# Another written-out order for a gated linear attention with a maxout layer

## The chip, the core and the metric

The kernel runs on one core of a Trainium2 chip. A core has TensorE (PE, the matmuls), VectorE (DVE), ScalarE (ACT) and GpSimd (POOL), each with an instruction stream of its own that runs in its own order; the streams wait for each other by semaphores. All DMAs of this kernel are issued by SyncE (SP), also in one order. The time is that of the device for one execution, in microseconds (us). The kernel before takes 144.04 us (median of three runs, 143.94 to 144.6).

## The reference

There are four batches of 768 tokens and eight heads of 48 channels. For each head a state of 48 x 48 is decayed by alpha, takes in the product of k and v, and is read by q. Then a layer takes the largest of three products of the 384 channels and multiplies it with a last weight:

```
for t in range(S):
    state = alpha[:, :, t, :, None] * state + einsum('bhd,bhe->bhde', k[:, :, t], v[:, :, t])
    y[:, :, t] = einsum('bhd,bhde->bhe', q[:, :, t], state)
x = y, heads side by side                    # 3072 x 384
h = maximum(maximum(x @ w1, x @ w2), x @ w3) # 3072 x 768
out = h @ w_out                              # 3072 x 384
```

## The kernel before

The tokens are worked through in 12 steps of 256 tokens (two units of 128); a step takes 256 tokens of one batch, and steps s and s+4 are neighbours in the same batch. Within a unit the recurrence is done in chunks by matmuls: the products of decayed q and k give a matrix of scores that is masked and multiplied with v, and the state that came into the unit adds its share. Two tokens at a time are folded into a pair, so the decay is summed over pairs. The maxout is done as x @ w1 + max(0, x @ (w2 - w1), x @ (w3 - w1)): the weights are subtracted once, w1 @ w_out is multiplied once, and TensorE adds x @ (w1 @ w_out) to the product of the maxima with w_out.

Nothing schedules the work at run time. A string, `ORDER`, lists about 760 pieces, and `emit` (line 538) issues each piece's instructions to their engines in that order. So the string sets, for each engine, the order of its own stream, the engine that does a movable piece, and the PSUM banks. A piece is written

```
k0v@3      piece k, index 0, on VectorE, of step 3   (v VectorE, p GpSimd, a ScalarE)
G2@4#7     piece G, index 2, of step 4, into PSUM bank 7
H5@0#3     five warming matmuls on a tile of zeros, into bank 3
```

The pieces, by the engine that they can go to, with the line of the instruction:

- SyncE: l loads alpha, q, k or v of a step in the index's order alpha 0, k 1, q 2, v 3 (line 102, 384 KB each, four buffers each); K loads a weight column group (118, 121); J loads the constants (130); D transposes q and k by a DMA (290, steps 5 to 11); W stores (500).
- ScalarE alone: N and r the logarithm of alpha and the inverse (209, 214, 216), e, f and g the decays from the sums (240, 250), I the row mask.
- TensorE: c sums the decays (231, 234), T transposes q and k (283, steps 0 to 4), A the scores (304), Y the outputs of a step (330), S the update of the state (388), B and P work on the weights (429, 440), G the gate products (452, six matmuls each), O the output products (486), H warming matmuls (505).
- VectorE alone: a the masks (319; 315 for step 0), the second maximum h1, h3, h5 (461), most state additions s (400).
- VectorE or GpSimd: m alpha products of a pair (205), u and w the near factors of k and q (219, 222), k and q the scaling by the decays (260), z the decay of the state (404), d the weight differences (418), M the gates between units (377).
- Any that can: x copies a step's outputs (162 or 164), v copies values by unit, y spreads the state, t copies what T made, b, n, C, p copy weights; h0, h2, h4 the first maximum (463 or 465), o scales an output (168 or 170), V scales v (168).

The weights are loaded into buffers of later steps: K0 to K7 lie in the third and fourth buffers of alpha, q, k and v, so that l0@2 can't be issued until K0 has been read. The waits between pieces follow from the tiles that they share. A piece that comes earlier in the string than another on the same engine runs earlier there; the string says nothing of the order between engines.

Of the kernel before, what the change touches and what calls it, by code (L numbers as in the profile page):

```python
# [23 lines left out]
def kernel(  # L24
# [513 lines left out]
    def emit(order):  # L538
# [21 lines left out]
        T1@2#5 t1v@2 K10@0 l1@4 h0a@1 b2a@0 G1@1#6 h1v@1 K11@0 K9@0 G3@1#1 l0@3 V0a@2 r0a@4 v1a@2 A1@2#3,7 a2v@2  # L560
        A0@2#0,2 a0v@2 a3v@2 S0@2#5,4 s0a@2 a1v@2 B2@0#6 n2v@0 G4@1#3 G4@0#0 G5@1#7 l0@5 z0p@2 l2@4 h3v@1 v0a@2
        Y0@2#5 x0v@2 Y2@2#2 y0a@2 Y3@2 x1a@2 M1p@0 u0p@4 k0v@4 G5@0#6 h4a@0 h5v@0 G5@2#1 l1@3 C2a@0 C0v@0 l2@3
        G4@2#5 l3@3 r1a@4 C1a@0 h4v@2 z1p@0 y1a@0 G0@2#2 m0v@3 s1v@2 h4a@1 G2@2#0 h2v@2 h5v@1 h5v@2 h0a@2 P0@0#6
        P1@0#5 N0a@3 r0a@3 p1a@0 w0v@4 q0v@4 c0@3#4 P2@0#3 e0a@3 m0p@5 G1@2#0 M0p@4 N0a@5 c0@5#7 f0a@3 r0a@5
        r1a@3 p0a@0 u0v@3 k0p@3 p2a@0 G3@2#1 h3v@2 f0a@5 T0@4#2 t0v@4 g0a@5 e0a@5 g0a@3 l3@4 T1@4#5 t1v@4 O0@0#6
        l0@7 l0@6 A1@4#3,1 h1v@2 V0a@3 a2v@4 M0p@5 w0p@3 q0v@3 A0@4#2,7 o0a@0 l1@5 S0@3#4,5 s0a@3 M1p@1 M0v@3
        z0p@3 l1@6 l2@5 O1@0#0 a1v@4 r1a@5 V0a@4 a3v@4 s1v@3 T0@3#3 t0v@3 o1a@0 T1@3#6 t1a@3 z1p@1 O0@1#4 m0p@7
        a0v@4 o0v@1 l0@8 y0a@3 N0a@7 A1@3#7,1 A0@3#5,3 l3@5 v0a@3 S0@4#0,6 W0@0 s0v@4 a1v@3 a0v@3 a2v@3 v0p@4
        m0p@6 N0a@6 O0@2#2 v1a@3 y1a@1 w0v@5 o0a@2 z0p@4 u0p@5 s1v@4 c0@7#4 v1p@4 c0@6#0 O1@1#3 r0a@7 o1a@1
        g0a@7 l0@9 g0a@6 Y3@3#5 a3v@3 Y2@3 Y0@3#7 r0a@8 x0a@3 Y0@4#2 Y2@4#6 l1@7 y0p@4 Y1@4 Y3@4 x1v@4 x0v@4  # L570
        O1@2#3 o1v@2 m0v@8 k0v@5 f0a@6 W1@0 l2@6 G0@4#1 h0v@4 e0a@6 x1a@3 M0p@6 G4@3#7 h4v@3 G2@3#6 G1@3#2
        G3@3#3 h2v@3 h3v@3 G4@4#1 l3@7 W0@2 q0p@5 D0@5 V0a@5 f0a@7 M1p@2 v1a@5 r1a@8 r0a@6 u0p@6 N0a@8 m0p@9
        r1a@6 c0@8#0 G0@3#5 e0a@8 h0a@3 r1a@7 h1v@3 G5@3#7 h5v@3 w0p@6 k0p@6 q0v@6 l3@6 D1@5 G5@4#6 G3@4#3 N0a@9
        V0a@7 h4a@4 h5v@4 e0a@7 c0@9#5 f0a@9 e0a@9 M1p@3 g0a@8 u0p@7 G2@4#2 h2a@4 f0a@8 g0a@9 M0p@8 G1@4#7 h1v@4
        O0@3#1 z1v@2 y1a@2 h3v@4 S0@5#6,4 s0v@5 k0p@7 r0a@9 A0@5#2,0 a1v@5 D1@6 W0@1 D0@6 z0v@5 A1@5#5,7 a2v@5
        a3v@5 o0a@3 V0a@6 l2@7 W0@3 O1@3#3 a0v@5 o1v@3 O1@4#6 y0a@5 o1a@4 r1a@9 v0p@7 v0p@5 Y0@5#0 Y1@5 v0v@6
        s1v@5 x0v@5 Y2@5#5 Y3@5 x1a@5 l0@10 S0@7#7,1 M1p@4 M0p@7 z1p@3 s0v@7 z0p@7 W1@1 l3@8 A1@6#2,3 a2v@6
        a3v@6 A0@6#6,4 a1v@6 S0@6#0,5 s0v@6 G2@5#7 G3@5#2 h2a@5 h3v@5 a0v@6 y0a@7 w0p@7 M1p@5 q0p@7 l1@8 D0@7
        D1@7 l2@8 G4@5#3 h4a@5 G1@5#4 G0@5#0 h0v@5 m0p@10 N0a@10 y1p@3 M0p@9 G5@5#7 O0@4#2 o0a@4 z1p@4 z0p@6
        y0a@6 c0@10#6 e0a@10 f0a@10 h1v@5 h5v@5 O1@5#3 O0@5#0 v1v@7 v1v@6 Y2@6#2 l0@11 s1v@6 u0v@8 k0v@8 g0a@10  # L580
        M1v@6 M0v@10 V0a@8 o1a@5 v0v@8 Y3@6 x1v@6 Y1@6#4 Y0@6 l2@9 r0a@10 S0@8#7 A0@7#5,6 s1v@7 a1v@7 s0v@8
        A1@7#3,2 a3v@7 a0v@7 a2v@7 x0a@6 G2@6#1 h2a@6 G3@6#6 h3v@6 G5@6#7 W1@3 G0@6#2 h0v@6 w0p@8 y1a@4 m0p@11
        z0p@8 N0a@11 W0@4 Y3@7#5 Y2@7 x1v@7 l1@9 W1@2 l3@9 Y0@7#3 Y1@7 x0a@7 c0@11#4 e0a@11 q0p@8 D0@8 D1@8
# [12 lines left out]
        h4a@11 h4a@10 G5@10#1 G2@11#5 h5v@10 o1a@8 W1@8 G3@11#0 h2v@11 h3v@11 W0@8 G0@11#2 h0v@11 G1@11#3 h1v@11
        G5@11#4 O1@10#7 O2@11#1 o1a@10 W1@10 h5v@11 O0@10#6 o0a@10 O3@11 o0v@11 O4@11#5,0 W0@10 W0@11 O5@11
        o1a@11 W1@11 O6@11 o2v@11 W2@11
    """

    blank = hTs[NH - 1].rearrange("p j m -> p (j m)")[:, :512]
# [34 lines left out]
```

## Time and profile before

| | us |
|---|---|
| median of the runs | 144.04 |
| the profiled execution | 143.54 |
| its span, first to last instruction | 141.8 |
| TensorE busy | 132.4 |
| VectorE busy | 113.7 |
| ScalarE busy | 95.5 |
| GpSimd busy | 73.8 |

The span is 1.7 us shorter than the profiled execution's time, since the launch and the end of the program lie outside it. Busy times of different engines lie beside each other. A view by time gives a start, a duration, the engine, the line, the operation and its tiles, and in brackets how long the engine had been idle before and what released it. TensorE's clock is granted by a throttle, and the profile gives it as a share of full speed.

### The profile page before, as it was taken

Reading aid. Unit: us, or ns where it says so; the run is one execution under the profiler, and the core shown is the slowest. Engines: PE = TensorE matmul, PEld = TensorE weight load, DVE = VectorE, ACT = ScalarE, POOL = GpSimd, SP = SyncE. Lnnn points to the kernel's source line nnn. Section 1 sums busy time; section 2 is a strip of 40 time slices with the busy share of each in tenths; the row PEclk is TensorE's granted clock in tenths of the full one; section 3 lists DMA queues with packets and bytes.
Section 4 is the critical chain, followed back from the end, with each engine's and each line's share of the span. In section 5 each row is a group of like instructions: output and inputs, shape, how many; then the busy total and the mean of one; then the engine's idle time right before and its main releaser. Section 6 shows DMA issues by size and latency. Waiting matters only on the chain.

```text
span 141.8 us, 5323 instructions
## 1 busy us (share of the span) xinstructions
PE 132.4 (93%) x2236; PEld 96.6 (68%) x2236; DVE 113.7 (80%) x215; ACT 95.5 (67%) x202; POOL 73.8 (52%) x107
## 2 busy tenths in 40 slices
PE   6988887999999999979999999899999999999990
PEld 2434556798868675768758858687678865788770
DVE  5466979989997999498999899977789879866711
ACT  3496798999899989996975486497375541344111
POOL 8217078257335399759495935888629643200000
PEclk9999996899999999999999999999999999999999
DMA  4999999999999998969999999998997955620214
GB/s 107 312 344 325 306 332 269 277 333 361 263 271 249 282 310 253 322 201 109 219 204 274 254 190 332 320 143 182 202 260 199 196 112 161 244 97 16 96 72 150
DMA packets 73031, 32.42 MB, mean 229 GB/s; under 512 B 65456, under 2 KB 73008, under 8 KB 73008
## 3 DMA queue, kind: packets, MB, share of 16 engines
q1 hardware_dynamic: 73008, 32.09, 86.4%
q8 instruction: 17, 0.28, 0.8%
q14 instruction: 6, 0.05, 0.1%
HBM read 23.69 MB, written 4.72 MB: 200 GB/s over the span
## 4 chain that ended last, share of the span: by engine, by line
PE 75%; SPq 8%; DVE 7%; DMA 4%; ACT 2%; issue 2%; DVEq 0%
PE bank L452 32%; PE bank L486 23%; PE bank L330 8%; SPq L102 5%; DMA rv<-in_v_dram 4%; PE bank L304 4%; PE bank L388 2%; SPq L118 2%; PE bank L440 2%; PE bank L283 2%; DVE lat L319 1%; DVE hT L461 1%; ACT qkT L162 1%; DVE qk L260 1%; PE bank L231 1%
## 5 line engine op out<-in xcount | busy, mean ns | idle before, releaser
L452 PE MATMUL bank<-xT,wdif 128*128 128x256 f16 x432 | 50.8, 275 | 0.8 <-DVE h L463 0.8
L452 PEld LDWEIGHTS <-wdif 128*128 128x128 f16 x432 | 41.4, 98 | 6.8 <-issue 1.1
L319 DVE TENSOR_TENSOR lat<-bank,cb 128x512 f16<-128x512 f32 x44 | 28.0, 681 | 1.3 <-PE bank L304 1.2
L461 DVE TENSOR_TENSOR hT<-bank,h 128x512 f16<-128x512 f32 x36 | 23.9, 685 | 6.2 <-PE bank L452 3.2
L486 PE MATMUL bank<-wo,hT 128*128 128x384 f16 (+1 forms) x150 | 27.5, 320 | 0.0
L486 PEld LDWEIGHTS <-hT 128*128 128x128 f16 x150 | 14.5, 98 | 8.9
L168 ACT ACTIVATE ob<-bank,ca 128x384 f32<-128x384 f32 (+1 forms) x18 | 10.3, 570 | 14.2 <-PE bank L486 12.9
L465 ACT ACTIVATE h<-bank 128x512 f16<-128x512 f32 x21 | 12.2, 599 | 8.1 <-PE bank L452 7.8
L486 PE MATMUL bank<-w1o,xT 128*128 128x384 f16 (+1 forms) x75 | 15.9, 321 | 0.0
L260 POOL TENSOR_TENSOR qk<-rk,ic 128x768 f16<-128x768 f32 x6 | 11.5, 1920 | 4.7 <-DVE rk L219 3.3
L505 PE MATMUL bank<-hT 128*128 128x512 f16 x42 | 12.7, 440 | 1.4 <-DVE hT L603 1.2
L168 ACT ACTIVATE vt<-rv,ca 128x768 f16<-128x768 f32 x12 | 11.3, 945 | 3.2 <-DMA rv<-in_v_dram 3.2
L162 ACT CAST xT<-bank 128x384 f16<-128x384 f32 x16 | 7.5, 480 | 7.1 <-PE bank L330 7.1
L222 POOL TENSOR_TENSOR rq<-rq,ic 128x384 f32<-128x384 f32 x8 | 8.0, 999 | 7.4 <-DMA rq<-in_q_dram 4.3
L463 DVE TENSOR_SCALAR h<-bank 128x512 f16<-128x512 f32 x15 | 9.9, 680 | 1.2 <-PE bank L452 1.2
L164 POOL COPY vu<-vt 64x384 f16<-64x384 f16 x14 | 7.3, 520 | 5.2 <-ACT vt L168 4.7
L205 POOL TENSOR_TENSOR ra<-ra 128x384 f32<-128x384 f32 x7 | 7.5, 1075 | 3.3 <-DMA ra<-in_alpha_dram 3.2
L162 ACT CAST st<-kept 64x192 f16<-64x192 f32 x26 | 9.0, 347 | 0.3
L260 POOL TENSOR_TENSOR qk<-rq,ac 128x768 f16<-128x768 f32 x5 | 9.1, 1814 | 0.1
L330 PE MATMUL bank<-lat,vu 128*32 128x128 f16 x352 | 8.3, 224 | 0.8 <-issue 0.7
L486 PEld LDWEIGHTS <-xT 128*128 128x128 f16 x75 | 6.5, 98 | 3.1
L505 PEld LDWEIGHTS <-hT 128*128 128x128 f16 x42 | 4.2, 110 | 6.4 <-issue 3.2
(80 smaller groups left out, 219.2 us busy)
## 6 DMA issues: line engine op xcount, KB each, us to landing
ra<-in_alpha_dram SPq DMA_DIRECT2D x12, 384.0 KB, 5.3
rk<-in_k_dram SPq DMA_DIRECT2D x12, 384.0 KB, 5.3
rq<-in_q_dram SPq DMA_DIRECT2D x12, 384.0 KB, 5.3
rv<-in_v_dram SPq DMA_DIRECT2D x12, 384.0 KB, 5.7
out_dram<-ob SPq DMA_DIRECT2D x23, 192.0 KB, 3.2
wst<-in_moe_w_out_dram SPq DMA_DIRECT2D x3, 384.0 KB, 7.2
ra<-in_moe_w_dram SPq DMA_DIRECT2D x2, 384.0 KB, 5.9
rk<-in_moe_w_dram SPq DMA_DIRECT2D x2, 384.0 KB, 5.5
```

The costliest lines, as they stand in the source:

```text
L162: nc.scalar.copy(out=dst, in_=src)
L168: nc.scalar.mul(dst, src, col)
L222: engines[eng].tensor_mul(raw("q", s, 0), raw("q", s, 0), decays["k"][s % 3][:, 0])
L260: engines[eng].tensor_mul(dst, src, by)
L319: nc.vector.tensor_mul(lats[s % 2][u][:, i], bank(("aps", s, u, i), [HP, P]), pmask.unsqueeze(1).broadcast_to([P, HP, P]))
L330: nc.tensor.matmul(y[x][C * m:C * (m + 1), f, :], lhs, rhs, start=(s, x, m) not in begun, stop=(seen[x] or U * (s // B) + x == 0) and n == ...
L452: nc.tensor.matmul(gps[:, j, :], wdif[:, f, g, jj * P:(jj + 1) * P], xT[:, f].rearrange("p u t -> p (u t)"), start=(f == 0), stop=(f == NF ...
L461: nc.vector.tensor_max(hTs[s % NH][:, 2 * jg:2 * jg + 2, :], gps, h)
L463: nc.vector.tensor_scalar_max(h, gps, 0.0)
L465: nc.scalar.activation(out=h, in_=gps, func=AFT.Relu)
L486: nc.tensor.matmul(ops, lhs, (w1o if what == "x" else wo16)[:, j, cols], start=((what, j) == every[0]), stop=((what, j) == every[-1]))
L505: nc.tensor.matmul(wps, blank[:, :P], blank, start=True, stop=True)
```

## The change

The string is replaced as a whole; the program around it is the same. The same pieces of work are in it (45 warming matmuls in place of 42). What differs is the place of each piece in its engine's stream, the banks, and the engine of some sixty movable pieces. The new string comes from a further search, which works each candidate through in the order of time and lets VectorE and GpSimd exclude each other, the one that is there first going ahead.

The engine's share of the movable pieces changes as follows (pieces before and after):

```
            VectorE    GpSimd    ScalarE
k            6 -> 9     6 -> 3
q            7 -> 8     5 -> 4
d            2 -> 4     4 -> 2
u            7 -> 5     5 -> 7
w            4 -> 5     8 -> 7
v            7 -> 4     7 -> 9     8 -> 9
z            4 -> 6    16 -> 14
M            3 -> 7    17 -> 13
y                       5 -> 7    13 -> 11
x            8 -> 5               16 -> 19
h           51 -> 50              21 -> 22
o            7 -> 5               18 -> 20
s           17 -> 16               3 -> 4
b            0 -> 2                3 -> 1
n            2 -> 1                1 -> 2
```

The first part of the string, the parts around the later steps that are named below, and the end, before (-) and after (+):

```diff
     ORDER = """
-        l0@0 m0v@0 r0a@0 N0a@0 r1a@0 J1@0 l1@0 u0v@0 H15@0#0 c0@0#0 e0a@0 k0v@0 K0@0 b0a@0 f0a@0 J0@0 I0a@0
-        H5@0#1 B0@0#1 l2@0 w0v@0 g0a@0 q0v@0 H6@0#2 T0@0#2 M0p@0 l0@1 m0p@1 r0a@1 N0a@1 K2@0 d1v@0 H3@0#3 c0@1#3
-        e0a@1 g0a@1 K1@0 d0p@0 r1a@1 T1@0#4 t1v@0 t0a@0 H3@0#5 H2^t1@0#5 A1@0#5,6 l1@1 u0v@1 k0v@1 l2@1 w0v@1
-        f0a@1 q0v@1 A0@0#7,0 a0v@0 a2v@0 a1v@0 l3@0 a3v@0 n0a@0 V0a@0 l3@1 V0a@1 v1p@1 v0p@1 K3@0 H5@0#4
-        S0@0#4,2 T0@1#3 t0a@1 T1@1#7 t1a@1 H2@0#5 S0@1#5,0 b1a@0 s0v@1 s0a@0 l0@2 m0v@2 N0a@2 K4@0 H1@0#6
-        A0@1#6,1 a0v@1 a1v@1 A1@1#3,7 a3v@1 M0p@1 z0p@1 y0a@1 a2v@1 z0p@0 d2p@0 y0a@0 B1@0#5 n1v@0 K5@0 d3v@0
-        s1v@0 l0@4 m0v@4 l2@2 c0@2#4 l1@2 g0a@2 M0p@2 Y0@0#6,1 x0a@0 Y3@0 x1a@0 K7@0 K6@0 r0a@2 r1a@2 w0p@2
-        Y2@1#7 Y3@1 x1a@1 s1v@1 f0a@2 d4p@0 G1@0#3 N0a@4 l3@2 K8@0 d5p@0 Y0@1#5 u0v@2 e0a@2 q0v@2 G0@0#2 h0a@0
...
-        z0p@8 N0a@11 W0@4 Y3@7#5 Y2@7 x1v@7 l1@9 W1@2 l3@9 Y0@7#3 Y1@7 x0a@7 c0@11#4 e0a@11 q0p@8 D0@8 D1@8
...
-        G3@7#6 G4@7#4 h4v@7 l3@10 h2v@7 h5v@7 h3v@7 O0@6#7 o0a@6 O1@6#0 D1@9 A0@8#2,3 a0v@8 A1@8#4,1 a2v@8 o1v@6
...
-        o1a@7 W1@7 G3@10#3 x1a@11 G0@10#5 G2@10#2 o0v@8 G1@10#0 h0v@10 G4@10#7 h1v@10 h2a@10 h3v@10 G4@11#4
-        h4a@11 h4a@10 G5@10#1 G2@11#5 h5v@10 o1a@8 W1@8 G3@11#0 h2v@11 h3v@11 W0@8 G0@11#2 h0v@11 G1@11#3 h1v@11
-        G5@11#4 O1@10#7 O2@11#1 o1a@10 W1@10 h5v@11 O0@10#6 o0a@10 O3@11 o0v@11 O4@11#5,0 W0@10 W0@11 O5@11
-        o1a@11 W1@11 O6@11 o2v@11 W2@11
+        K0@0 b0v@0 J0@0 H13@0#0 B0@0#0 l0@0 l0@1 J1@0 m0p@0 m0v@1 l1@0 l2@0 I0a@0 K1@0 N0a@0 H6@0#1 c0@0#1 r0a@0
+        l1@1 n0v@0 K2@0 f0a@0 e0a@0 r0a@1 l2@1 u0v@0 k0v@0 l3@1 N0a@1 r1a@0 w0v@0 H6@0#2 c0@1#2 e0a@1 q0v@0
+        H5@0#3 T1@0#3 l3@0 d0v@0 g0a@1 T0@0#4 u0v@1 t1a@0 t0a@0 d1v@0 l0@2 k0v@1 g0a@0 l0@4 f0a@1 H2@0#5
+        H2^t1@0#5 A0@0#5,6 r1a@1 K3@0 V0a@1 w0v@1 q0v@1 A1@0#7,0 a2v@0 H5@0#3 S0@1#3,4 T1@1#1 K4@0 v0p@1 K5@0
+        V0a@0 m0p@2 l2@2 a1v@0 a3v@0 l1@2 t1a@1 s0a@1 T0@1#2 t0v@1 S0@0#7,6 s0a@0 M0v@1 H2@0#0 A1@1#0,1 z0p@1
+        N0a@2 M0v@0 z0v@0 A0@1#3,2 y0a@0 K6@0 a0v@0 s1v@0 v1p@1 y0a@1 a0v@1 H2@0#7 Y3@0#7 Y0@0#5 a3v@1 r0a@2
+        r1a@2 K7@0 c0@2#6 s1v@1 b1v@0 H2@0#3 B1@0#3 x0a@0 m0p@4 N0a@4 d2v@0 x1a@0 c0@4#1 g0a@4 g0a@2 M1p@0 d3v@0
+        l3@2 a1v@1 e0a@2 G2@0#4 G0@0#5 f0a@2 n1a@0 M0p@2 M0p@4 K8@0 a2v@1 G1@0#7 e0a@4 l2@4 h0a@0 u0v@2 k0v@2
+        Y0@1#2 x0a@1 Y2@1#6 Y3@1 x1a@1 G3@0#3 l0@3 G0@1#0 r0a@4 r1a@4 h0a@1 w0p@2 q0v@2 G2@1#5 b2a@0 h1v@0
+        T1@2#2 h2v@1 h2a@0 f0a@4 d4p@0 t1v@2 T0@2#6 B2@0#0 G1@1#7 h3v@0 V0a@2 t0v@2 n2a@0 K10@0 l1@4 G3@1#5
...
+        c0@11#2 G3@6#6 a3v@7 o1a@5 a2v@7 Y3@7#0 w0v@8 Y2@7 o0a@5 Y0@7#7 Y1@7 x1a@7 q0v@8 D0@8 G5@6#1 x0a@7
+        G0@7#5 G3@7#3 g0a@11 e0a@11 y1a@4 D1@8 G1@7#0 w0p@9 q0p@9 v0p@8 k0v@9 h4a@6 V0a@9 h3v@6 z0v@8 G4@7#7
+        r1a@10 h0v@7 h5v@6 f0a@11 W0@5 G2@7#4 h2a@7 G5@7#6 M0v@10 h4v@7 W0@4 v0p@9 O1@6#5 D0@9 l2@10 r0a@11
+        r1a@11 h3v@7 y0a@8 v1a@8 h5v@7 h1v@7 A0@8#1,2 a0v@8 A1@8#4,7 D1@9 S0@9#3 z1p@5 y1a@5 s0v@9 O0@6#6 l1@10
...
+        G0@8#5 D1@10 h3v@8 G5@9#0 h0a@8 G1@9#7 k0v@11 l3@11 w0v@11 h1v@8 G3@9#4 v0a@10 o0a@7 G2@9#5 h2a@9 h5v@8
+        G0@9#3 q0v@11 D1@11 G4@9#1 h0a@9 O0@8#5 A1@10#2,3 h1v@9 h4a@9 h5v@9 h3v@9 D0@11 S0@10#7 s0v@10 A0@10#1,0
+        a0v@10 a1v@10 O1@9#4 W1@3 V0a@11 z0p@10 y0p@10 W0@7 M1p@7 O0@9#7 a3v@10 o0a@8 W0@8 z1v@7 y1p@7 a2v@10
+        W1@6 S0@11#1 o0a@6 A1@11#0,3 s0v@11 z0p@11 A0@11#5,2 a3v@11 Y2@10#6 Y1@10#1 Y0@10 x0v@10 Y3@10 x1v@10
+        O1@8#3 o1a@9 o0v@9 W0@9 G5@10#1 a1v@11 G4@10#6 G2@10#4 a2v@11 a0v@11 Y1@11#7 v1a@11 v0a@11 Y0@11 h4v@10
...
+        y0p@11 Y3@11#2 x0a@11 Y2@11 x1a@11 G3@10#0 h5v@10 G0@10#5 G2@11#6 G3@11#7 G0@11#2 h0a@10 h2a@10 h3v@10
+        W0@6 o1a@8 G1@10#1 G1@11#5 G4@11#4 h2v@11 h1v@10 O1@10#0 h3v@11 h4a@11 G5@11#3 W1@8 h0v@11 h1v@11
+        O2@11#6 h5v@11 o1a@10 W1@7 W1@10 W1@9 O0@10#1 o0v@10 O3@11 o0a@11 O4@11#7,4 O5@11 W0@11 W0@10 O6@11
+        o1a@11 W1@11 o2a@11 W2@11
     """
```

At the start the old string loads alpha of step 0 (l0@0) first, the new one the weight K0 and a constant (J0). In the new one GpSimd does the first alpha product (m0p@0) where VectorE did it, ScalarE copies both transposed halves of step 0, and the first gate group is G2@0 where it was G1@0.

## The prediction

> **What bounds the kernel now.** I read the page's engine totals first, then the slices with the granted clock, then the chain that ended last.
>
> ```profile
> PE 132.4 (93%) x2236; PEld 96.6 (68%) x2236; DVE 113.7 (80%) x215; ACT 95.5 (67%) x202; POOL 73.8 (52%) x107
> ...
> PEclk9999996899999999999999999999999999999999
> ...
> PE 75%; SPq 8%; DVE 7%; DMA 4%; ACT 2%; issue 2%; DVEq 0%
> ```
>
> TensorE is busy 93% of 141.8 us, and three quarters of the chain lie on it. Both orders have the same matmuls, apart from three warming ones, so only what stands around them can change: the start, until the first gate matmuls (L452, pieces G) run without a break; TensorE's waits in the body; the end. I cut the span there.
>
> ```profile
> 0.00:24.80 24.80, 20.77 (x335) 11.27 (x336) 17.92 (x42) 17.51 (x35) 12.51 (x27) 0.96 0.99 285
> 24.80:28.60 3.80, 3.80 (x45) 2.81 (x42) 3.47 (x7) 3.59 (x9) 1.00 (x1) 0.84 0.96 276
> 28.60:138.30 109.70, 107.82 (x1863) 82.54 (x1860) 91.91 (x167) 74.12 (x160) 60.29 (x79) 1.00 0.86 217
> 138.30:141.80 3.50, 0.02 (x1) 0.00 (x0) 0.42 (x1) 0.31 (x1) 0.00 (x0) 1.00 0.42 142
> ```
>
> The columns are the stretch and its length, then busy time of TensorE, its weight loads, VectorE, ScalarE and GpSimd, then granted clock, DMA share and GB/s. In the body TensorE stands for only 109.70 - 107.82 = 1.9 us; no reordering can win more there. The start is 24.8 us in which warming matmuls (L505) fill up a TensorE that has little to do, at a DMA share of 0.99. So the possible gain is 1.9 us in the body and whatever the start gives; the possible loss is open, with VectorE busy 84% of the body (91.91 of 109.70).
>
> The largest body wait is this one, in the views by time of TensorE, VectorE and GpSimd:
>
> ```profile
> 63.66 0.82 PE L452 MATMUL bank<-xT,wdif 128*128 128x256 f16 x6 [0.77 <-DVE h L463]
> ```
> ```profile
> 61.26 1.75 DVE L260 TENSOR_TENSOR qk<-rk,ic 128x768 f16<-128x768 f32 x1
> ```
> ```profile
> 60.88 1.32 POOL L205 TENSOR_TENSOR ra<-ra 128x384 f32<-128x384 f32 x1
> ```
>
> VectorE's scaling of k took 1.75 us while GpSimd multiplied alpha until 62.2; the same form takes 0.96 us when it is alone (row of 7.54, below). So 0.79 us of a VectorE instruction went with an overlap, and TensorE's 0.77 us wait at 63 is its price. This is what the new search is told to see.
>
> **The change, part by part.** First the moves between engines; the costs are these groups by form.
>
> ```profile
> L260 POOL TENSOR_TENSOR qk<-rk,ic 128x768 f16<-128x768 f32 x6 | 11.5, 1920 | 4.7 <-DVE rk L219 3.3 <-PE bank L452 1.4
> L260 DVE TENSOR_TENSOR qk<-rk,ic 128x768 f16<-128x768 f32 x6 | 6.5, 1085 | 0.9 <-ACT ic L240 0.8
> ...
> L164 POOL COPY vu<-vt 64x384 f16<-64x384 f16 x14 | 7.3, 520 | 5.2 <-ACT vt L168 4.7
> ...
> L164 DVE CAST xT<-bank 128x384 f16<-128x384 f32 x8 | 4.3, 550 | 2.0 <-PE bank L330 2.0
> ...
> L164 DVE COPY vu<-vt 64x384 f16<-64x384 f16 x14 | 3.8, 274 | 0.4
> ```
>
> Three more k scalings go from GpSimd to VectorE: +3 x 1.085 and -3 x 1.92. Two weight differences (L418) follow them; as they have the same 128x768 shape I price them like k: +2.2 and -3.8. Three unit copies (two instructions each) leave VectorE, two for GpSimd and one for ScalarE: -6 x 0.274 = -1.6, and +4 x 0.52 = +2.1 on GpSimd. Three x copies leave VectorE for ScalarE: -3 x 0.55. The other moves (two u and two o away from VectorE, two z, two b, one q and one w towards it, some gates) go both ways in single pieces and I take them as nothing. Net: VectorE 3.3 + 2.2 - 1.6 - 1.7 = +2.2 us, GpSimd -5.8 - 3.8 + 2.1 = -7.5 us. On the path this costs nothing while VectorE has its 109.70 - 91.91 = 17.8 us of body slack; without that cover it would cost TensorE 2.2 us.
>
> A rule speaks against this move. The Trainium skill (SBUF — State Buffer, "Who interferes with whom") says that a VectorE instruction with two SBUF inputs and a GpSimd instruction that reads SBUF exclude each other, the later one blocked for the whole of the earlier. By it each scaling brought to VectorE is one more that can be blocked; the 1.75 us row agrees. By the rule the six or so more such instructions, with GpSimd busy about half the time and half a 1.0 us instruction in front, would add an estimated 6 x 0.5 x 0.5 = 1.5 us to VectorE, where the trace's mean of 1.085 already holds such overlaps; either sum stays within the slack.
>
> **The start** is a chain of transfers. ScalarE and VectorE by time show when loads landed, in the bracket of the wait that they ended, and what one piece takes:
>
> ```profile
> 4.23 0.53 ACT L214 ACTIVATE ic<-ra 128x384 f32<-128x384 f32 x1 [2.22 <-DMA ra<-in_alpha_dram]
> ```
> ```profile
> 13.38 1.01 ACT L162 COPY qkT<-bank 128x1024 f16<-128x1024 f16 x1
> ```
> ```profile
> 17.21 0.94 ACT L168 ACTIVATE vt<-rv,ca 128x768 f16<-128x768 f32 x1 [0.53 <-DMA rv<-in_v_dram]
> ```
> ```profile
> 4.47 0.49 DVE L205 TENSOR_TENSOR ra<-ra 128x384 f32<-128x384 f32 x1
> 6.19 0.56 DVE L219 TENSOR_TENSOR rk<-rk,ra 128x384 f32<-128x384 f32 x1 [1.22 <-DMA rk<-in_k_dram]
> 7.54 0.96 DVE L260 TENSOR_TENSOR qk<-rk,ic 128x768 f16<-128x768 f32 x1 [0.80 <-ACT ic L240]
> ...
> 11.11 1.09 DVE L418 TENSOR_TENSOR wdif<-rk,ra 128x768 f16<-128x768 f32 x1 [0.74 <-DMA rk<-in_moe_w_dram]
> ...
> 17.00 2.47 DVE L315 TENSOR_TENSOR lat<-bank,rowmask 128x512 f16<-128x512 f32 x4
> ```
>
> Alpha of step 0 (l0@0) is first in the queue and lands at 4.23; v of step 1 (l3@1) has ten loads of 384 KB and two constants (a quarter of a load together) ahead and lands at 17.21. So one load takes (17.21 - 4.23) / 10.26 = 1.27 us, and a load lands at about 4.2 + 1.27 x (loads ahead). The new order puts the weight K0 and a constant ahead of l0@0: it lands at 4.2 + 1.27 x 1.17 = 5.7, l1@0 at 8.4, K2 at 13.4 (seven loads and both constants ahead), l3@0 at 17.3, K4 at 22.3. VectorE's first work is now halving K0, behind its clearing; GpSimd's first is step 0's alpha product (1.08 us, the mean of its L205, against 0.49 on VectorE); ScalarE begins with the row mask, which waits for the constant, and the logarithm stands behind it.
>
> Nothing queued behind these waits is wanted earlier: behind K0's halving VectorE has step 1's alpha product, and l0@1 lands at 7.0. On the queue l0@2 takes K0's place in memory, so it waits for the second difference (14.5 by the walk below) with K3, K4 and K5 behind it; the loads issued by then keep the DMA busy until 17.3, so I take no gap.
>
> Walked on with these durations: product done 6.8; logarithm and two decays, three ScalarE steps of about 0.5 us like the row at 4.23, and the sums between them 8.7; k scaled 9.9, q scaled 11.6 (1.2 us later than before), transposed 12.1. Both copies (t1, t0) are now ScalarE's, 2 x 0.95: 14.0, when the scores start. That matches before's 14.45:
>
> ```profile
> 14.45 0.65 PE L304 MATMUL bank<-qkT 48*64 48x128 f16 x32 [0.19 <-ACT qkT L162]
> ...
> 22.29 1.37 PE L330 MATMUL bank<-lat,vt 64*32 64x128 f16 x64
> ...
> 24.78 1.43 PE L452 MATMUL bank<-xT,wdif 128*128 128x256 f16 x6
> ...
> 26.48 2.14 PE L452 MATMUL bank<-xT,wdif 128*128 128x256 f16 x18
> ```
>
> VectorE meanwhile owes two differences and step 1's u, k, w, q. The second difference waits for K2 until 13.4, so these end at 13.4 + 1.09 + 0.96 + 0.56 + 0.96 = 17.0; three masks (0.62 each) to 18.8, a copy, step 0's state (V of l3@0 to 18.2, its update, ScalarE's t1@1 and two copies) to 20.1, the last mask to 20.8. Step 0's outputs (L330 x64) then run from 20.8 instead of 22.29. Before G2, its first G, VectorE still has two states, two masks, the halving of K3 and the difference of K3 and K4, some 2.5 + 1.1 us: 24.4. K4's landing at 22.3 is hidden by that. Three G at 0.67 run to 26.4, the masks of step 1 end at 26.7, its outputs at 27.2, the fourth G at 27.9, with one more set of sums already done. Before, the same four G end at 28.6. So I take -0.9 us here. The bounds: one load more ahead of K4 or K5 costs +1.3, and running the Gs with no wait for the masks gives -1.6. The three more warming matmuls lie before the first G, where TensorE waits anyway: nothing.
>
> **Body:** the 0.77 wait goes: -0.8. The other 1.1 us I leave in place, with between 0 and 1.9 + 2.3 (the transposes below) as bounds of the whole. **Queue and end:** the loads stand earlier against their consumers (l2@10 and l2@11 stood right at them, now 5.3 us of TensorE work ahead), on a queue where the transposes (L290) block what stands behind. After the last gate group stand O2@11 and O0@10 (16 matmuls) ahead of the one that needs its maximum; the last two scalings are both ScalarE's, but the last store waits for the issue of the one before it anyway. Nothing.
>
> Sum: 143.54 (the profiled run, 141.8 of span and 1.7 around it) - 0.9 - 0.8 = 141.8. The median of the runs is 0.5 above the profiled run, so 142.3. A measurement tells 0.5%, 0.7 us, from no change.
>
> **Rivals.**
> Slower: the transposes by DMA come late.
>
> ```profile
> L290 SPq DMA_TRANSPOSE qkT<-qk x14: 1237/1330/2278, 63.2 to 115.2; - x14
> ```
> ```profile
> DMA to landing us min/median/max: 3.1/4.0/6.0
> ```
>
> Two issues and a landing are 2 x 1.33 + 4.0 = 6.7 us, at most 2 x 2.28 + 6.0 = 10.6. Between the end of step 8's q scaling and its scores the new order lists 6.4 us of TensorE work (old 8.5), at step 11 6.6 (6.9). At the median that is 0.3 us of wait, at the worst 4.2 and 4.0. It decides once the two waits together pass 2.4 us, since 142.3 + 2.4 is 144.7; at half the worst, 4.1, the time is 146.4, and at 3 us 145.3. Against it: no such wait stands in the old profile, whose tightest step had 6.6. Chance 0.25 with other late work of that size.
>
> Same: half clock falls on the gates. In 24.80 to 28.60 the granted clock is 0.84, and six matmuls took 1.43 where eighteen then took 2.14. If the new start, with TensorE idler between 15 and 20 us, puts a whole half-clock stretch (two slices of 3.5 us, digits 6 and 8) on its first Gs, up to 1.7 us of work is lost, of which 1.1 is new beyond the 0.6 lost now: 143.4. Chance 0.15. The Trainium skill (TensorE: Matmul & The Clock Gate, "Part 1: The HAM clock gate") has a free-running activity window of 3.4 us; by it, too, the place of the slow stretch is not set by the order alone.
>
> The change doesn't do what it says: overlaps on the shared access go from one place to another. 143.1, only the start's gain. Chance 0.12. Best case: start -1.6 and all 1.9 of the body: 140.6. Chance 0.08. My forecast has 0.40.
>
> **How the numbers follow.** Faster: 0.40 + 0.08 + half of 0.12 + a little of the clock's = 0.57; same 0.18; slower 0.25. The range takes in the best case and the transposes at 3 us: 140.6 to 145.3. The forecast's own, 141.6 to 143.1.
>
> **What would show it.** Right: first G near 24.4, outputs of step 0 near 21, TensorE's idle time between the start's end and the last matmul near 1.1 us, no VectorE scaling of 1.7 us ahead of a TensorE wait, GpSimd near 66 us busy. Wrong: first Gs after 25.5, waits before L304 from step 8 on, or VectorE's row naming TensorE's waits at several masks (L319) or maxima (L461).

## The result, and the profile after

The new order is slower, by about 1%. Its 22 runs have a median of 145.68 us (143.61 to 147.54), the 22 runs of the old order beside them 143.94 us (142.15 to 146.51); the ratio is 1.0105 with a 95% interval of 1.0066 to 1.0144. The forecast was 142.3 us, faster; the measured median lies above the upper end of its range, 145.3. Ratios, here and below, leave out the executions that lie more than 1.5% above the fastest of their kernel, so they are not the quotients of the medians that stand beside them. Single executions of either kernel differ by up to 3%, so I judge by ratios of many runs and read a profile for where, not for how much.

The profiled execution took 145.67 us, with a span of 143.9 us (before: 143.54 and 141.8). Its page, the same rows as shown of before:

```profile
span 143.9 us, 5327 instructions
...
PE 133.0 (92%) x2239; PEld 95.5 (66%) x2239; DVE 119.2 (83%) x214; ACT 97.6 (68%) x206; POOL 69.8 (49%) x104
...
PEclk9999999999999999999999999999999999999998
```

VectorE is busy 5.5 us longer with one instruction less, and GpSimd 4.0 us shorter. The granted clock has no slow slice in the start this time, so the clock is not where time went. The stretches, with columns as in the prediction (busy time of TensorE, weight loads, VectorE, ScalarE, GpSimd, then clock, DMA share, GB/s), cut at the last matmul of this execution:

```profile
0.00:24.80 24.80, 20.66 (x311) 10.53 (x312) 18.64 (x46) 16.40 (x34) 9.70 (x23) 1.00 0.99 284
24.80:28.60 3.80, 3.80 (x73) 3.09 (x72) 3.32 (x6) 3.68 (x11) 1.77 (x4) 1.00 0.93 262
28.60:140.50 111.90, 108.54 (x1858) 81.85 (x1856) 97.19 (x164) 77.02 (x162) 58.33 (x77) 1.00 0.84 213
140.50:143.90 3.40, 0.00 (x0) 0.00 (x0) 0.00 (x0) 0.53 (x2) 0.00 (x0) 0.84 0.50 170
```

The loss is in the body. It lasts 111.9 us where it lasted 109.7; TensorE idles 3.4 us of it (before 1.9), and VectorE is busy 97.2 us of it (before 91.9). The end is unchanged (3.4 and 3.5 us). Of the 2.2 us that the body is longer, 1.5 are idle time; the other 0.7 lie in rows that count as TensorE's busy time, and no run here says why. TensorE's waits in the body, by time (start, duration, engine, line, operation; in the brackets the idle time ahead of it and its releaser):

```profile
65.76 2.78 PE L452 MATMUL bank<-xT,wdif 128*128 128x256 f16 x24 [0.34 <-DVE hT L461]
...
71.03 0.42 PE L304 MATMUL bank<-qkT 48*64 48x128 f16 x16 [0.58 <-DVE hT L461]
71.62 0.41 PE L304 MATMUL bank<-qkT 48*64 48x128 f16 x15 [0.18 <-DVE hT L461]
...
97.54 0.82 PE L452 MATMUL bank<-xT,wdif 128*128 128x256 f16 x6 [0.65 <-DVE hT L461]
98.67 0.65 PE L486 MATMUL bank<-w1o,xT 128*128 128x384 f16 x3 [0.32 <-DVE h L463]
...
106.81 0.35 PE L330 MATMUL bank<-lat,vu 128*32 128x128 f16 x12 [0.78 <-DVE lat L319]
```

All six, 2.85 us together, end on VectorE. So VectorE is the engine that came late, in two stretches, 63 to 72 us and 91 to 107 us, although it has 111.9 - 97.2 = 14.7 us of slack over the body. Cut at the same times, TensorE idles 1.15 us between 60 and 92 us (before 1.47) and 1.75 us between 92 and 124 us (before 0.30); so beside the old order, which has waits of its own in the first of these stretches, it is the second that costs this execution most. What VectorE did in both, in its own view by time:

```profile
63.54 1.17 DVE L377 TENSOR_TENSOR gm<-ge,ge 128x4 f32<-128x4 f32 x1
...
66.22 2.16 DVE L205 TENSOR_TENSOR ra<-ra 128x384 f32<-128x384 f32 x1
...
91.89 1.33 DVE L222 TENSOR_TENSOR rq<-rq,ic 128x384 f32<-128x384 f32 x1
93.26 2.45 DVE L260 TENSOR_TENSOR qk<-rq,ac 128x768 f16<-128x768 f32 x1
95.63 1.25 DVE L260 TENSOR_TENSOR qk<-rk,ic 128x768 f16<-128x768 f32 x1
...
105.59 0.56 DVE L222 TENSOR_TENSOR rq<-rq,ic 128x384 f32<-128x384 f32 x1 [1.58 <-DMA rq<-in_q_dram]
```

and GpSimd's beside it:

```profile
62.28 2.40 POOL L260 TENSOR_TENSOR qk<-rq,ac 128x768 f16<-128x768 f32 x1
...
66.16 1.81 POOL L260 TENSOR_TENSOR qk<-rk,ic 128x768 f16<-128x768 f32 x1
...
91.81 1.01 POOL L222 TENSOR_TENSOR rq<-rq,ic 128x384 f32<-128x384 f32 x1 [1.97 <-DMA rq<-in_q_dram]
92.89 2.00 POOL L260 TENSOR_TENSOR qk<-rq,ac 128x768 f16<-128x768 f32 x1
94.84 3.55 POOL L164 COPY vu<-vt 64x384 f16<-64x384 f16 x4
```

The first row of VectorE is M1v@3, a product of four numbers a partition. Alone it takes 0.15 us; here it ends at 64.71, right after GpSimd's q0p@6 has ended at 64.68. The second, m0v@9, takes 0.55 us alone and 2.16 beside k0p@6, and ends 0.4 us after it. In the other stretch w0v@8 and q0v@8 stand against w0p@9 and q0p@9, and k0v@9 against GpSimd's copies. Each time VectorE's instruction reads two operands from SBUF, and GpSimd is in an instruction of its own that started earlier. The Trainium skill (SBUF — State Buffer, "Who interferes with whom") states this as an exclusive lock on a shared pair of ports, held for the whole instruction by whichever was first; the rows agree, down to an instruction of four elements that stands for a microsecond.

The same in VectorE's groups by form (times, busy us, mean ns), after:

```profile
L260 DVE TENSOR_TENSOR qk<-rk,ic 128x768 f16<-128x768 f32 x9 | 9.9, 1103 | 0.3
L260 DVE TENSOR_TENSOR qk<-rq,ac 128x768 f16<-128x768 f32 x8 | 9.9, 1238 | 0.2
L205 DVE TENSOR_TENSOR ra<-ra 128x384 f32<-128x384 f32 x5 | 4.4, 898 | 2.4 <-DMA ra<-in_alpha_dram 2.4
...
L377 DVE TENSOR_TENSOR gm<-ge,ge 128x4 f32<-128x4 f32 x2 | 1.3, 663 | 0.0
```

Before, the q scaling had a mean of 981 ns over seven, and alpha's product 656 ns over five. I add up, for every VectorE form that reads and writes SBUF alone, count times (mean less the duration when nothing overlaps: 0.955 us for a scaling, 0.53 for alpha's product, 0.155 for M and so on). This blocked time is 3.8 us before and 8.7 us after. So of VectorE's 5.5 us more, 4.9 are spent standing still, and only 0.6 are work.

The four pieces that stood ahead of these waits, M1@3, m0@9, w0@8 and q0@8, were all on GpSimd in the old order; the new string brought them to VectorE. The net table of the moves hides this: alpha's products (m) are five on VectorE before and after, though not the same five. Counted piece by piece, 109 pieces change their engine, not some sixty, and 48 of them change between VectorE and GpSimd, 29 towards VectorE.

### The profile page after: what moved, and what is told of

It is laid out like the page before. It is cut to its first block, busy times and chain, and to the rows that moved or that the text cites. A ratio compares the mean times of both kernels' runs of the same rounds, so it can differ in the third digit from the quotient of the medians.

```text
span 143.9 us, 5327 instructions
## 1 busy us (share of the span) xinstructions
PE 133.0 (92%) x2239; PEld 95.5 (66%) x2239; DVE 119.2 (83%) x214; ACT 97.6 (68%) x206; POOL 69.8 (49%) x104
## 5 line engine op out<-in xcount | busy, mean ns | idle before, releaser
L461 DVE TENSOR_TENSOR hT<-bank,h 128x512 f16<-128x512 f32 x36 | 23.7, 684 | 5.2 <-ACT h L465 3.9
L486 PEld LDWEIGHTS <-hT 128*128 128x128 f16 x150 | 14.5, 98 | 8.9
L164 POOL COPY vu<-vt 64x384 f16<-64x384 f16 x18 | 11.1, 614 | 14.2 <-ACT vt L168 13.4
L505 PE MATMUL bank<-hT 128*128 128x512 f16 x45 | 13.9, 445 | 1.4 <-DVE hT L603 1.2
L162 ACT CAST xT<-bank 128x384 f16<-128x384 f32 x19 | 8.6, 488 | 6.6 <-PE bank L330 6.6
L260 DVE TENSOR_TENSOR qk<-rk,ic 128x768 f16<-128x768 f32 x9 | 9.9, 1103 | 0.3
L260 DVE TENSOR_TENSOR qk<-rq,ac 128x768 f16<-128x768 f32 x8 | 9.9, 1238 | 0.2
L304 PE MATMUL bank<-qkT 48*64 48x128 f16 x384 | 8.9, 219 | 1.1 <-DVE hT L461 0.8
L404 POOL TENSOR_TENSOR kept<-fa,gm 128x192 f32<-128x192 f32 x8 | 4.0, 506 | 11.6 <-DVE fa L400 10.8
L162 ACT COPY vu<-vt 64x384 f16<-64x384 f16 x18 | 9.2, 511 | 0.3
L219 POOL TENSOR_TENSOR rk<-rk,ra 128x384 f32<-128x384 f32 x7 | 7.0, 1002 | 4.7 <-DMA rk<-in_k_dram 4.7
```

The lines of the kernel that those rows point to most:

```text
L162: nc.scalar.copy(out=dst, in_=src)
L164: engines[eng].tensor_copy(out=dst, in_=src)
L260: engines[eng].tensor_mul(dst, src, by)
L304: nc.tensor.matmul(aps[i][to * J:(to + 1) * J, a * U + n, :], qkT[rows, r, 1, p, cols], qkT[rows, :, 0, p, cols], start=True, stop=True)
L461: nc.vector.tensor_max(hTs[s % NH][:, 2 * jg:2 * jg + 2, :], gps, h)
L486: nc.tensor.matmul(ops, lhs, (w1o if what == "x" else wo16)[:, j, cols], start=((what, j) == every[0]), stop=((what, j) == every[-1]))
```

## The experiments

Two theories. The first: exclusion, a handful of VectorE instructions that meet a long GpSimd instruction in a stretch where TensorE has no reserve. The second: VectorE simply has more to do, or the start or the queue is to blame (where an expectation has a theory 3, it is late loads). All edits but the splices of two orders are on single pieces of the string, and all ratios are to the old kernel; the new order stands at 1.0105.

**Take GpSimd's instruction away.** VectorE keeps every piece; the two scalings of step 6 on GpSimd are left out, so step 6 computes with the scaled q and k that stood in their buffers.

```diff
-        h1v@3 G4@4#4 w0p@6 q0p@6 y1p@3 V0a@6 h4a@3 G5@3#1 h5v@3 M1p@4 k0p@6 r0a@9 f0a@8 h2a@4 G0@4#7 l1@7 m0v@9
+        h1v@3 G4@4#4 w0p@6 y1p@3 V0a@6 h4a@3 G5@3#1 h5v@3 M1p@4 r0a@9 f0a@8 h2a@4 G0@4#7 l1@7 m0v@9
```

> The new order without GpSimd's two scalings of step 6 (q0p@6 and k0p@6 are left out, so step 6 goes on with the scaled q and k of step 2). VectorE keeps every instruction. Theory 1 (exclusion: a VectorE instruction with two SBUF inputs waits for the GpSimd instruction that is there first): the VectorE gate product that took 1.17 us at 63.54 takes 0.16, the alpha product that took 2.16 at 66.22 takes about 0.55, and TensorE's waits at 65.76 (0.34), 71.03 (0.58) and 71.62 (0.18) go: 1.1 us less than the new order, ratio to the old kernel about 1.003. Theory 2 (VectorE has simply too much work in the new order): VectorE's work is the same, the waits stay, ratio 1.010.

Median 143.95 us, ratio 1.0011 (0.9963 to 1.0059): nearly all of the loss is gone. The two VectorE instructions in this kernel's trace (its profiled execution took 146.19 us, with a wait of 1.09 us for a weight difference near 37 us and a slow clock behind it, so I read it only from 60 us on):

```profile
66.99 0.15 DVE L377 TENSOR_TENSOR gm<-ge,ge 128x4 f32<-128x4 f32 x1
...
69.17 0.55 DVE L205 TENSOR_TENSOR ra<-ra 128x384 f32<-128x384 f32 x1
```

and its stretches (columns as above), where TensorE is now busy 31.82 and 31.64 us of 32; the new order has 30.85 and 30.25 there:

```profile
60.00:92.00 32.00, 31.82 (x631) 24.60 (x631) 29.27 (x58) 24.77 (x56) 18.26 (x28) 1.00 1.09 230
92.00:124.00 32.00, 31.64 (x566) 23.80 (x568) 27.93 (x47) 21.75 (x43) 15.57 (x22) 1.00 1.01 225
```

VectorE's list of work is the same, so its amount of work isn't the cause. The later stretch became tight as well, without an edit there: in this execution GpSimd's w0p@9 had its load only at 95.43, and by then w0v@8 and q0v@8 had run undisturbed, 0.54 and 0.96 us at 94.14 and 94.72. So which pieces meet depends on when a load lands, too; in the new order's profile GpSimd had waited 1.97 us for that load and started at 91.81, just ahead of VectorE. This run also takes 4.4 us off GpSimd's busy time, so it doesn't show by itself what of the gain is the first stretch's own.

**Move VectorE's side, stretch by stretch.** The two blocked pieces of the first stretch go back to GpSimd, where they queue behind the scaling instead of standing beside it:

```diff
-        ... h2v@3 M1v@3 z1v@3 e0a@8 ... l1@7 m0v@9
+        ... h2v@3 M1p@3 z1v@3 e0a@8 ... l1@7 m0p@9
```

> The new order with the two blocked VectorE pieces handed to GpSimd in their places (M1@3, m0@9), which puts them behind the scalings that blocked them. Theory 1: the three waits of TensorE between 65 and 72 go, 1.1 us less, ratio 1.003. Theory 2: VectorE is relieved of 0.6 us of work at its undisturbed durations, so at most 0.6 us, ratio 1.006. Theory 3 (late loads set the new order's loss): no change, 1.010.

144.18 us, 1.0059 (1.0016 to 1.0103). The time is the 1.006 of theory 2, and the interval takes in all three theories, so here only the trace tells them apart: the waits ahead of the scores (L304) are gone, and of the one ahead of the gates 0.15 us is left. (In this execution too w0v@8 and q0v@8 ran undisturbed, 0.55 and 0.96 us, ahead of GpSimd's start at 93.08.) But in VectorE's view the block isn't gone as a whole; it has passed on to the next piece with two inputs, z1v@3, which takes 0.36 us alone:

```profile
64.58 1.37 DVE L404 TENSOR_TENSOR kept<-fb,gm 128x192 f32<-128x192 f32 x1
```

For the second stretch, the two pieces of step 8:

```diff
-        c0@11#2 G3@6#6 a3v@7 o1a@5 a2v@7 Y3@7#0 w0v@8 Y2@7 o0a@5 Y0@7#7 Y1@7 x1a@7 q0v@8 D0@8 G5@6#1 x0a@7
+        c0@11#2 G3@6#6 a3v@7 o1a@5 a2v@7 Y3@7#0 w0p@8 Y2@7 o0a@5 Y0@7#7 Y1@7 x1a@7 q0p@8 D0@8 G5@6#1 x0a@7
```

> The new order with w0@8 and q0@8 handed to GpSimd, ahead of its w0@9 and q0@9, which blocked them on VectorE (1.33 and 2.45 us at 91.89 and 93.26). Theory 1: the waits at 97.54 (0.65) and 98.67 (0.32) go; the transposes of step 8 are issued near 93 in place of 95.8, so q of step 10 behind them on the queue comes earlier and the wait of 0.78 at 106.8 goes too: 1.7 us less, ratio 0.998. Theory 2: VectorE is relieved of 1.35 us, so the first two waits go, 1.0 us, and the third stays: 1.003. If GpSimd is too slow for step 8's transposes, a wait before its scores (L304) near 100 takes their place: 1.005 to 1.01.

143.76 us, 1.0026 (0.9986 to 1.0066). By the time alone this is again theory 2's 1.003, and theory 1's 0.998 lies just outside the interval; but theory 2 kept the wait of 0.78 us, and it is gone. TensorE has no wait between 90 and 110; those at 65 to 72 remain. This stretch has a second link, the queue. In SP's view of the new order the transposes of step 8 wait for q0v@8, which ends at 95.71, and behind them in the one queue stands l2@10, the load for which VectorE waited 1.58 us at 105.59:

```profile
95.77 2.63 SPq L290 DMA_TRANSPOSE qkT<-qk  x2
...
99.68 1.26 SPq L290 DMA_TRANSPOSE qkT<-qk  x1
100.99 0.58 SPq L102 DMA_DIRECT2D rq<-in_q_dram  x1
```

With q0 of step 8 on GpSimd, in the same view, all of it is 2.5 to 2.7 us earlier:

```profile
93.09 2.78 SPq L290 DMA_TRANSPOSE qkT<-qk  x2
...
97.15 1.25 SPq L290 DMA_TRANSPOSE qkT<-qk  x1
98.45 0.58 SPq L102 DMA_DIRECT2D rq<-in_q_dram  x1
```

So w0v@10 was a victim. Taking it alone out of VectorE's stream tells how much of the loss hangs on that last link:

```diff
-        o1a@6 O1@7#0 o1a@7 l1@11 l3@10 a1v@8 z0v@9 a2v@8 y0p@9 O0@7#1 w0v@10 q0p@10 W1@4 v1a@9 Y3@8#3 a3v@8 Y2@8
+        o1a@6 O1@7#0 o1a@7 l1@11 l3@10 a1v@8 z0v@9 a2v@8 y0p@9 O0@7#1 w0p@10 q0p@10 W1@4 v1a@9 Y3@8#3 a3v@8 Y2@8
```

> The new order with only w0@10 handed to GpSimd. On VectorE it waited 1.58 us for its load (to 105.59) with the last mask of step 8 behind it, and TensorE waited 0.78 us for that mask. Theory 1 with theory 3 (the late load is a part of the loss, by way of the queue that q0@8's blocking held up): that wait goes, 0.8 us less than the new order, ratio 1.005; the waits at 65 to 72 and 97 to 99 stay. If the mask is late for another reason: 1.010.

144.72 us, 1.0048 (1.0005 to 1.0092). Of the six waits only the 0.78 us one at 106.81 is gone, and the one at 97.54 is down to 0.35; the gain of 0.57%, 0.8 us, is about that size, with an interval as wide as the gain.

**Both stretches.** The four pieces of the first two edits together:

> Both hand-overs together. Theory 1: the gains add, 2.8 us less than the new order, ratio 0.991, faster than the old kernel; VectorE busy near 112 us in place of 119.2. Theory 2: 1.6 us less, ratio 0.999. If something else takes over as the late piece, ratio 1.000 to 1.005.

142.36 us (141.32 to 144.25), ratio 0.9927 (0.9889 to 0.9965): better than both kernels, and clear of theory 2's 0.999. Its page and its body, by stretches:

```profile
PE 131.3 (94%) x2239; PEld 95.2 (68%) x2239; DVE 114.2 (82%) x210; ACT 97.3 (70%) x206; POOL 73.3 (52%) x108
```

```profile
28.60:136.50 107.90, 106.98 (x1854) 81.28 (x1851) 91.41 (x159) 76.36 (x161) 61.90 (x81) 1.00 0.88 218
```

TensorE's waits from 28 us on, in all (us, times, longest):

```profile
PE bank L452 <- POOL wdif L418: 0.3, 1, 0.3
PE bank L231 <- ACT la L209: 0.2, 1, 0.2
```

None is VectorE's. z1v@3 is blocked here as well (1.37 us at 62.96), without a wait of TensorE behind it. Four pieces of about 760 are back on an engine that is half idle, and VectorE's busy time fell by 5.0 us, of which their own work is 0.55 + 0.15 + 0.55 + 0.955 = 2.2 us; GpSimd's rose by 3.5.

**Was the old order's one wait an exclusion too?** There the alpha product m0v@8 and k0v@5 stand against GpSimd ahead of the 0.77 us wait at 63.66:

```diff
- m0v@8
+ m0p@8
```

> The old order with m0@8 handed from VectorE to GpSimd in its place. It stood there between GpSimd's u0@6 and m0@9 and in front of k0@5, at 60 to 63 us. Theory 1 (exclusion): the two VectorE instructions that took 1.14 and 1.75 us, 1.4 us over their undisturbed time, lose one piece and its overlap, TensorE's 0.77 wait at 63.66 goes and nothing else: ratio 0.995. If the old body's waits are not set by such overlaps: 1.000.

143.35 us, 0.9953 (0.9909 to 0.9997), so just clear of no change. The wait is gone in TensorE's view, the gates run through from 60.05:

```profile
60.05 4.09 PE L452 MATMUL bank<-xT,wdif 128*128 128x256 f16 x36
```

although k0v@5 itself is blocked as before, in VectorE's view, since GpSimd's u product starts at 60.67:

```profile
60.79 1.70 DVE L260 TENSOR_TENSOR qk<-rk,ic 128x768 f16<-128x768 f32 x1
```

So what helped was one alpha product less for VectorE ahead of the same place (1.14 us at 60.19 in the old trace), not that the scaling went free. It was enough for the 0.77 us that the place lacked. This execution had another wait in its place, 1.67 us at 105.13 ahead of a state update, for values whose load came late.

**Is the start a gain, as forecast?** The new order's first 138 pieces (up to G3@0), then the rest in the order of the old string, no bank changed:

```diff
-        K0@0 b0v@0 ... G2@0#4 ... G3@0#3   then the new string's remaining pieces
+        K0@0 b0v@0 ... G2@0#4 ... G3@0#3   then the old string's remaining pieces, in its order
```

> The new order up to and with G3@0 (its first 138 pieces), then every piece that is left in the order, on the engines and in the banks of the old one. If the loss lies in the body (both profiles have the same four gate groups done at 28.6 us): ratio to the old kernel 1.000, within 0.003. If the new start is worth the 0.9 us of the prediction: 0.994. If the loss lies in the start or in what it leaves behind for the queue: 1.005 to 1.010.

143.18 us, 0.9954 (0.9919 to 0.9988): by this run the start gains about 0.65 us (0.2 to 1.2), and the loss is not there. TensorE's first gate group in its trace:

```profile
24.33 2.13 PE L452 MATMUL bank<-xT,wdif 128*128 128x256 f16 x18
```

With the old kernel's one body wait taken off in the same way (m0v@8 to m0p@8):

> The new start, the old body, and m0@8 on GpSimd. If the two gains (0.9954 and 0.9953) are of different places they multiply: 0.991, and TensorE's wait for VectorE near 63 us (0.8) goes. If the start's gain came from that place too: 0.995.

143.09 us, 0.9978 (0.9941 to 1.0015): no gain over the kernel without that edit, where I expected about 0.4% more. In this execution the same first 138 pieces had their first gates later:

```profile
25.57 2.13 PE L452 MATMUL bank<-xT,wdif 128*128 128x256 f16 x18
```

From that group to the last matmul are 112.5 us, against 112.8 without the edit: of the 0.77 us wait some 0.3 shows up as a gain in these two profiles, and the rest does not. The start alone differed by 1.24 us between the two, with the same instructions up to there. The two intervals overlap, so I leave open whether the edit is worth something on top of the new start, and how much of the start's gain would stand in more runs.

**The other way round.** The old string's first 135 pieces, then the new body:

> The other way round: the old order up to and with G3@0 (135 pieces), then what is left as the new order has it. Loss in the body: ratio 1.010, with VectorE's blocked instructions of 1.2 to 2.5 us and TensorE's waits for VectorE between 60 and 107 still there. Loss in the start: 1.000 to 1.003.

146.59 us (six runs), 1.0213 (1.0146 to 1.0280). It can't be read as a sum, for the seam makes a wait of its own in TensorE's view, a transpose into a bank that the other start still holds:

```profile
31.60 0.61 PE L283 MATMUL bank<-cb,qk 128*128 128x128 f16 x8 [1.64 <-ACT h L465]
```

But of the new body's blocked instructions those of the first stretch are there behind the other start too, in VectorE's view, and w0v@8 and q0v@8 of the second (the last two rows) are not:

```profile
64.28 1.17 DVE L377 TENSOR_TENSOR gm<-ge,ge 128x4 f32<-128x4 f32 x1
...
66.96 2.16 DVE L205 TENSOR_TENSOR ra<-ra 128x384 f32<-128x384 f32 x1
...
93.00 0.54 DVE L222 TENSOR_TENSOR rq<-rq,ic 128x384 f32<-128x384 f32 x1
93.57 0.96 DVE L260 TENSOR_TENSOR qk<-rq,ac 128x768 f16<-128x768 f32 x1
```

Other banks for ten pieces behind the seam (the expectation says eleven) should have taken its wait away; the changed pieces alone:

```diff
-        G2@1#5 T0@2#6 G1@1#7 G3@1#5 A0@2#2,3 Y0@2#3 G1@2#3 G4@2#7
+        G2@1#4 T0@2#5 G1@1#3 G3@1#4 A0@2#2,6 Y0@2#7 G1@2#7 G4@2#3
...
-        P1@0#7 A1@4#7,0
+        P1@0#3 A1@4#3,0
```

> The old start and the new body again, with other banks for eleven pieces right after the cut, since in the first splice TensorE waited 1.64 us at 31.6 for a bank, a wait that neither whole order has. If the new body alone makes the loss and the new start is a gain of about half a per cent (1.0105 / 0.9954): ratio 1.015, and that wait is gone. If the first splice's 1.021 is the body's own: 1.020. If start and body don't add up: 1.005 or less.

148.45 us (six runs), 1.0365 (1.0315 to 1.0414). That wait went, and others came, the largest in TensorE's view:

```profile
35.52 0.42 PE L304 MATMUL bank<-qkT 48*64 48x128 f16 x16 [1.39 <-DVE lat L319]
```

Both splices fail as a test of the start; what is known of it comes from the run with the new start and the old body.

**Can more be had?** On the kernel with the four moves, the piece that inherited the block goes to GpSimd too, and an alpha product comes back:

```diff
- m0p@6 ... z1v@3
+ m0v@6 ... z1p@3
```

> The new order with both hand-overs (M1@3, m0@9, w0@8, q0@8) and two pieces more: z1@3, which took up the block that M1@3 had (1.37 us), goes to GpSimd, and m0@6, GpSimd's product that blocked k0@3 for 0.8 us near 44 us, goes to VectorE, behind k0@3. Theory 1: VectorE's blocked time falls by another 1.8 us, but TensorE has no wait for VectorE left in that kernel's body, so the time gains little: 0.990 to 0.993. Theory 2 (time follows VectorE's total): another 1 per cent, 0.983.

143.38 us, 0.9954 (0.9906 to 1.0003): not better than the four moves alone; the interval takes in most of theory 1's 0.990 to 0.993 and leaves out theory 2's 0.983. Alpha's product m0v@6 is now itself blocked, in VectorE's view:

```profile
44.79 1.36 DVE L205 TENSOR_TENSOR ra<-ra 128x384 f32<-128x384 f32 x1
```

and TensorE waits for a mask at a place where it had none:

```profile
104.70 0.35 PE L330 MATMUL bank<-lat,vu 128*32 128x128 f16 x12 [1.21 <-DVE lat L319]
```

That mask stood behind a load, in VectorE's view, the same l2@10 as in the new order:

```profile
103.49 0.56 DVE L222 TENSOR_TENSOR rq<-rq,ic 128x384 f32<-128x384 f32 x1 [2.48 <-DMA rq<-in_q_dram]
```

Whether the two edits made that load late isn't shown.

## Why the prediction was wrong

**The failing step is "on the path this costs nothing while VectorE has its 109.70 - 91.91 = 17.8 us of body slack".** The slack is a sum over 110 us, and the moves landed in two stretches, of 9 and 16 us, where TensorE's next matmuls wait for VectorE's maxima and masks: there 2.6 and 2.3 us of blocking came through as 1.10 and 1.75 us of waits. That slack was still 14.7 us in the new order while VectorE made TensorE wait six times. The sentence went on "without that cover it would cost TensorE 2.2 us". That the last matmul came 2.1 us later is luck: the 2.2 us were the price of other pieces, as work.

**The size +2.2 us for VectorE was wrong too, and the pieces that cost were not in it.** Busy time rose by 5.5 us there and fell by 4.0 on GpSimd, forecast +2.2 and -7.5. The gates, the q and the w are among "the other moves" that I took "as nothing" by their net counts, and alpha's product moved without any change of the count; M1v@3, q0v@8, w0v@8 and m0v@9 are such pieces. I priced the moved scalings at the old mean of 1.085 us, which holds the old overlaps, and so took blocking for a property of the form. It is one of the place: VectorE's work rose by 0.6 us, its blocked time by 4.9. The sentence on the Trainium skill (SBUF — State Buffer, "Who interferes with whom") put 1.5 us on blocking by GpSimd's average share. The rule agrees with these traces; the average was what failed, since four meetings alone, M1v@3, m0v@9, w0v@8 and q0v@8, cost (1.17 - 0.15) + (2.16 - 0.55) + (1.33 - 0.55) + (2.45 - 0.955) = 4.9 us. That this equals the rise of the whole sum is chance: all other meetings, old ones gone and new ones come, cancel.

**Body -0.8.** The old order's 0.77 us wait is gone in the new one, as forecast, and its cure alone is worth 0.5% in the old kernel (0.9953, up to 0.9997). But that the 0.79 us of overlap in one scaling was its price doesn't hold: with one alpha product less ahead of it the wait went while the scaling still took 1.70 us. "The other 1.1 us I leave in place" failed: 2.85 us of waits for VectorE came. I had argued that the search is told to see the exclusion, hence removes it. The blocked time more than doubled instead.

**The start, -0.9.** Right in sign by the run with the new start alone, 0.65 us; the second kernel with that start (0.9978, up to 1.0015) is not clear of no gain. In the profile after, the same four gate groups are done at 28.6 us as before, so nothing of it shows there but one set of sums that is done earlier. First gates were forecast at 24.4; nine executions with the new start had them between 24.33 and 25.68, the profiled one at 25.00. Outputs of step 0 began at 21.64 in it (their row of 64 at 22.29, as before), not at 20.8: my walk had the masks and states too early. Of the clock, the rival "half clock on the gates" did not happen in the profile after. Two of the thirteen profiles, both with the old start, have slow slices at 21 to 28 us, one has its slow slice at 36 to 40 us, and the others have none before the end.

**Queue and end, nothing.** The end held. The queue did not: the place that I named for the slower rival, the transposes of step 8, is where one of the links lay, but neither cause nor victim was as told. The transposes came late because q0v@8 was blocked, and what waited was the load behind them and by it VectorE, not the scores.

**The rivals.** "Overlaps go from one place to another" is the mechanism that came true, and I gave it 143.1 us, as if the price moved unchanged. With six waits at places without reserve it was 145.7. My slower rival had the right sign and the wrong cause. Of the signs that I listed for a wrong forecast one did appear: VectorE's maxima (L461) released four of the six waits. Of the signs of a right one, "no VectorE scaling of 1.7 us ahead of a TensorE wait" failed with the 2.45 us at 93.26.

Shown by runs: the loss is in the body, goes when GpSimd's side of the meeting goes (1.0011), and turns into a gain when VectorE's side of both stretches goes back to GpSimd (0.9927). With one stretch alone the medians lie between (1.0059, 1.0026), the first of them not clear of the new order's interval; there the traces carry the argument. Not settled: how often the meeting of step 8's two pieces happens, since the profiles of the new order, of the run with w0@10 moved and of the second splice have it, and those of three other runs that leave both pieces in place don't; why the edit on the old kernel's wait adds nothing to the new start, and how much of the run without step 6's scalings comes from GpSimd having less to do.

## What to carry to other kernels

Look up whether the engine that takes a piece has reserve at that place: cut the span into stretches of a few microseconds around the piece, and don't let an average slack stand for cover. Where two engines exclude each other, price an instruction by its duration alone plus the rest of whatever the other one is doing at that moment (on the four rows here this gives 1.29, 2.30, 1.48 and 2.59 us where 1.17, 2.16, 1.33 and 2.45 were measured). Count moves piece by piece, not net. After a change add up count times (mean less undisturbed duration) over the forms concerned; here that one sum, 3.8 against 8.7 us, pointed to the cause. Here four blocked pieces were cured by giving them back to the engine that blocked them, where they wait in line without holding up the other's stream; a fifth piece handed over, together with one moved the other way, gained nothing.

## What was not expected of the hardware

- A VectorE product of 128 x 4 elements, 0.15 us alone, took 1.17 us behind a GpSimd scaling. Small size is no protection.
- The block is handed on: with that product gone, the next VectorE instruction with two SBUF inputs took 1.37 us in place of 0.36.
- GpSimd pays as well. Its q scaling took 2.40 us at 62.28, where VectorE's scaling of k was there first, against 1.81 for its k scaling at 66.16 in the same profile; four of its copies took 3.55 us together at 94.84, while VectorE scaled q and k, and 2.17 us in the kernel with step 8's two pieces on GpSimd.
- The same order doesn't meet in the same places each time. w0v@8 and q0v@8 took 1.33 and 2.45 us in the new order's profile, and 0.54 to 0.55 and 0.96 us in three of its variants that leave both in place.
- Up to the first gates, executions with the same instructions differ by more than a microsecond (24.33 to 25.68), as much as most of these edits are worth.
